# One transpose for both key blocks of an attention tile, split behind it by a triangular mask

## The chip, the core and the metric

The kernel runs on one core of one Trainium2 chip. The metric is the time of one execution on the device in microseconds (us); lower is better. The kernel before took 815.19 us, the median of three runs (814.88 to 815.65). One further execution was profiled; all views of the trace come from it.

The engines are named as in the profile: PE (matrix products and transposes; PEld is its loading of weights), DVE (the vector engine), ACT (the scalar engine), POOL (GpSimd) and SP (which issues transfers). Each engine works through its own list of instructions in order, and waits where an input or a free buffer is missing.

## The reference

Attention with a sliding window of 128 keys and 4 "sink" keys that are always seen, then a gated feed-forward block without a nonlinearity. Four sequences of 768 tokens, 8 heads of 64; model width 512, inner width 1536.

```python
scores = q @ k.T / sqrt(64)
keep   = (key < n_sink) | ((0 <= query - key) & (query - key < window))
a      = softmax(where(keep, scores, -1e9))
x      = (a @ v)                       # 8 heads side by side: 3072 x 512
out    = ((x @ w_a) * (x @ w_b)) @ w_out
```

## The kernel before, in words

**Tiling.** A q-tile is 128 queries, and a sequence has six of them. With a window of at most 128, the queries of tile t see the keys of key block t-1 ("A" below) and of block t ("B"), and the sinks. A tile of probabilities `p` is therefore 128 queries by 264 columns: 128 for A, 8 for the sinks, 128 for B. In A a key is in the window only where its place in its block is above the query's place in its tile; in B only where it is not above it. So at each of the 128 x 128 places at most one of A and B is not zero.

**Stages.** The work is cut into eight chunks (`CHUNKS`) of a sequence's q-tiles. For each chunk, `moe` computes the feed-forward block, and the attention of the next chunk is woven into it in small steps. The first two chunks use another path, `parts_exact`, in which the change touches nothing. The six others use `parts_split`, with three q-tiles each: three chunks hold the tiles 0 to 2 of a sequence ("first halves") and three the tiles 3 to 5 ("second halves"). With 8 heads that makes 24 units (head, tile) per chunk and 144 in all. A unit is in `late` when its tile is the third or a later one: one of three in a first half, all three in a second half, so 3 x 8 + 3 x 24 = 96 units.

**A unit, step by step** (lines of the kernel before): PE makes the scores (L396); DVE adds the mask and takes the row extreme (L401); ACT takes the exponential and its row sum (L403); DVE adds a small constant and inverts (L405, L406); ACT scales `p` (L407) and, in late units, copies the 8 sink columns out (L412). Two steps later PE transposes A and B, one instruction each (L428), into one PSUM tile `t`; ACT copies both to `pt` in the rounded format of the products (L431, called hi below), and DVE writes the remainder beside it (L432, lo). When a head's three units are there, PE multiplies them with the values (L444, `av`), five or seven products in the order of `GROUPS`; ACT and DVE add the two halves of the result into `xf` (L449 to L451). In each second half POOL prepares the next heads' operands (`ks`, `qh`, `ql`, `vv`: L322, L325), and in the feed-forward block it makes `gl` (L689).

**What sets the order.** A scheduler orders the program of each engine at build time, from its own estimates; at run time the order is fixed. Buffers that matter: four of `p`, one of `pt` for both hi and lo, one PSUM bank each for scores (`s`), transposes (`t`) and `av`.

## Time and profile before

| | before |
|---|---|
| median of 3 runs | 815.19 us |
| profiled execution | 814.39 us, of which the span of the trace is 812.5 us |
| PE busy | 788.8 us, 97% of the span |
| DVE, ACT, POOL busy | 53%, 59%, 47% |
| granted TensorE clock | 0.993 of full speed |
| attention of the six `parts_split` chunks | from 192 us to 712 us |

The attention of the second halves lies at 355 to 430, 450 to 525 and 637 to 712 us, that of the first halves at 192 to 249, 263.5 to 336 and 545.5 to 618 us. Line numbers (L428) are those of the kernel before. In a row, `out<-in` names tiles, then come sizes, the count, the summed busy time and the mean of one instruction in ns. A matrix instruction's time runs from its start to the landing of its last result, and the next one starts before that.

### The profile page before, as it was taken

To read this page: it belongs to the slowest core of one execution; us is meant where nothing else is said; L and a number is where in the kernel's file an instruction comes from. 1 tells how busy PE (TensorE), PEld (TensorE's weight loads), DVE (VectorE), ACT (ScalarE), POOL (GpSimd) and SP (SyncE) were. 2 spreads that over 40 slices of the span, in tenths; PEclk is the share of its full clock that TensorE was granted. 3 is DMA by queue.
4 is the path that set the end of the run, shared out by engine and by line. 5 is a ranking of instruction groups with operands and counts; after the bars stand their busy time and mean duration, and the time that the engine had idled before them with its cause. 6 is when DMAs were issued, how large, how long until landed. Compare 5 with 4: busy or idle time off the path is not lost.

```text
span 812.5 us, 13593 instructions
## 1 busy us (share of the span) xinstructions
PE 788.8 (97%) x4457; PEld 698.6 (86%) x4457; DVE 432.7 (53%) x1427; ACT 476.7 (59%) x1384; POOL 380.7 (47%) x483
## 2 busy tenths in 40 slices
PE   8997999999999999999999999999999999999995
PEld 5655777778989999999999999999999999999994
DVE  6889777834663555445654456535554456431001
ACT  5775665636774767467874677647765677631111
POOL 1248665673772564626653565506635366102110
PEclk9999899999999999999999999999999999999998
DMA  8866430031221133413323233221333132010001
GB/s 317 297 215 247 164 112 21 11 94 63 67 67 63 47 114 108 124 53 105 99 89 106 74 95 130 86 85 58 122 112 101 53 105 60 1 40 1 1 1 44
DMA packets 44784, 76.17 MB, mean 94 GB/s; under 512 B 4640, under 2 KB 24224, under 8 KB 44704
## 3 DMA queue, kind: packets, MB, share of 16 engines
q1 hardware_dynamic: 41648, 69.70, 26.5%
q10 hardware_dynamic: 3024, 5.51, 1.8%
q8 instruction: 37, 0.61, 0.3%
q14 instruction: 43, 0.35, 0.1%
q0 software_dynamic: 32, 0.00, 0.0%
HBM read 68.90 MB, written 6.29 MB: 93 GB/s over the span
## 4 chain that ended last, share of the span: by engine, by line
PE 85%; DVE 8%; ACT 3%; issue 2%; POOL 0%; DMA 0%; DVEq 0%; POOLq 0%; ACTq 0%
PE o L672 23%; PE a L663 23%; PE b L663 22%; PE t L428 4%; PE s L396 4%; PE av L444 3%; PE s L525 2%; PE av L579 1%; PE t L562 1%; PE t L579 1%; DVE p L539 1%; DVE wf_a L280 1%; DVE wf_a L278 1%; DVE g L684 1%; ACT p L403 1%
## 5 line engine op out<-in xcount | busy, mean ns | idle before, releaser
L663 PE MATMUL a<-xh,w_a 128*128 128x384 f32 (+2 forms) x768 | 218.9, 346 | 0.0
L663 PE MATMUL b<-xh,w_b 128*128 128x384 f32 (+2 forms) x768 | 215.3, 343 | 0.0
L672 PE MATMUL o<-w_o,gh 128*128 128x512 f32 x576 | 187.6, 406 | 0.0
L689 POOL TENSOR_TENSOR gl<-g,gh 128x384 fp32r<-128x384 f32 (+2 forms) x80 | 82.8, 1035 | 197.5 <-ACT gh L687 194.7
L663 PEld LDWEIGHTS a<-xh,w_a 128*128 128x128 f32 x768 | 138.8, 188 | 6.4 <-issue 1.5
L663 PEld LDWEIGHTS b<-xh,w_b 128*128 128x128 f32 x768 | 138.9, 188 | 4.5 <-issue 0.8
L684 DVE TENSOR_TENSOR g<-b,g 128x384 f32<-128x384 f32 (+2 forms) x96 | 53.4, 556 | 152.6 <-PE b L663 144.5
L663 PE MATMUL a<-xl,w_a 128*128 128x384 f32 (+2 forms) x384 | 129.3, 337 | 0.9 <-DVE xl L645 0.9
L663 PE MATMUL b<-xl,w_b 128*128 128x384 f32 (+2 forms) x384 | 129.1, 336 | 0.0
L672 PEld LDWEIGHTS o<-w_o,gh 128*128 128x128 f32 x576 | 104.6, 189 | 19.4 <-issue 1.0
L672 PE MATMUL o<-w_o,gl 128*128 128x512 f32 x288 | 114.0, 396 | 0.6 <-POOL gl L689 0.6
L687 ACT CAST gh<-g 128x384 fp32r<-128x384 f32 (+2 forms) x96 | 49.4, 514 | 80.9 <-DVE g L684 79.0
L680 ACT COPY g<-a 128x384 f32<-128x384 f32 (+2 forms) x96 | 45.2, 471 | 79.3 <-PE a L663 69.9
L407 ACT ACTIVATE p<-p,st 128x128 f32<-128x128 f32 (+1 forms) x144 | 71.4, 496 | 26.4 <-DVE st L406 25.5
L403 ACT ACTIVATE p<-p,st 128x128 f32<-128x128 f32 (+1 forms) x144 | 71.6, 497 | 8.4 <-DVE st L401 8.3
L663 PEld LDWEIGHTS a<-xl,w_a 128*128 128x128 f32 x384 | 72.5, 189 | 3.6 <-DVE xl L645 1.3
L663 PEld LDWEIGHTS b<-xl,w_b 128*128 128x128 f32 x384 | 72.5, 189 | 2.0 <-issue 0.3
L431 ACT CAST pt<-t 128x128 fp32r<-128x128 f32 (+1 forms) x144 | 50.4, 350 | 39.3 <-PE t L428 37.5
L432 DVE TENSOR_TENSOR pt<-t,pt 128x128 fp32r<-128x128 f32 (+1 forms) x144 | 57.2, 397 | 21.1 <-ACT pt L431 19.5
L672 PEld LDWEIGHTS o<-w_o,gl 128*128 128x128 f32 x288 | 54.3, 189 | 14.1 <-POOL gl L689 1.0
L322 POOL TENSOR_SCALAR qh<-qr 128x384 fp32r<-128x384 f32 x48 | 24.6, 512 | 75.8 <-PE s L396 48.1
L325 POOL TENSOR_TENSOR ks<-kr,ks 64x400 fp32r<-64x400 f32 (+1 forms) x48 | 57.6, 1200 | 3.9
(141 smaller groups left out, 1317.8 us busy)
## 6 DMA issues: line engine op xcount, KB each, us to landing
qr<-in_qT_dram SPq DMA_DIRECT2D x48, 192.0 KB, 2.6
raw_a<-in_wa_dram SPq DMA_DIRECT2D x12, 512.0 KB, 5.6
raw_b<-in_wb_dram SPq DMA_DIRECT2D x12, 512.0 KB, 6.3
raw_o<-in_wo_dram SPq DMA_DIRECT2D x12, 512.0 KB, 6.9
chk_a<-in_wa_dram SPq DMA_DIRECT2D x24, 256.0 KB, 2.8
chk_b<-in_wb_dram SPq DMA_DIRECT2D x24, 256.0 KB, 2.7
chk_o<-in_wo_dram SPq DMA_DIRECT2D x24, 256.0 KB, 2.7
out_dram<-os ACTq DMA_DIRECT2D x21, 256.0 KB, 2.1
```

The lines of the kernel that those rows point to most:

```text
L325: self.nc.gpsimd.tensor_tensor(o, i, high.bitcast(F32), op=ALU.subtract)
L396: nc.tensor.matmul(ps[:, :w], lhsT=q[:, i * P:(i + 1) * P], rhs=ks[:, c0:c0 + w], start=m == 0, stop=m == 1)
L403: nc.scalar.activation(p[:, :w], p[:, :w], AF.Exp, bias=st[:, 0:1], scale=-1.0, accum_out=st[:, 1:2])
L407: nc.scalar.mul(p[:, :w], p[:, :w], st[:, 3:4])
L431: nc.scalar.copy(hs, tp[:, :n, :])
L432: nc.vector.tensor_tensor(ls, tp[:, :n, :], hs.bitcast(F32), op=ALU.subtract)
L663: nc.tensor.matmul(ps[:, :n], lhsT=w[:, ksl], rhs=x[:, :n], start=kk == 0 and i == 0, stop=kk == NK - 1 and i == 2)
L672: nc.tensor.matmul(outs[i], lhsT=g[:, sl], rhs=w, start=j == 0 and k == 0, stop=j == NJ - 1 and k == 2)
L680: nc.scalar.copy(g[:, :n], pa[:, :n])
L684: nc.vector.tensor_tensor(g[:, :n], pb[:, :n], g[:, :n], op=ALU.mult)
L687: nc.scalar.copy(gh[:, :n], g[:, :n])
L689: e.tensor_tensor(gl[:, :n], g[:, :n], gh[:, :n].bitcast(F32), op=ALU.subtract)
```

## The change

In the 96 late units A and B are added before the transpose, which is possible since one of them is zero at each place. One transpose then carries both. Behind it they are separated: `ma` is a matrix of 0 and 1, with 1 where the key's place is above the query's; A is the transposed tile times `ma`, and B the transposed tile minus A. Both are written over `p`, in SBUF, and the hi copy and the lo remainder read them there and no longer in PSUM. The scaling is done on the 128 columns of the sum, and the 8 sink columns are scaled on their way out. The slots of `pt` are renumbered (`GROUPS`), the `av` products stay as many; `ma` is made once, by POOL, at the start.

```diff
-UNITS = ((0, 4, "BA"), (1, 2, "AB"), (3, 5, "AB"))
-GROUPS = ((0, 0, 2, 0), (1, 2, 2, 1), (2, 5, 0, 2), (-1, 4, 1, 0))
+GROUPS = ((0, 1, 2, 0), (1, 3, 2, 1), (2, 5, 0, 2), (-1, 0, 1, 0))
...
+        nc.gpsimd.memset(self.ma, 1.0)
+        nc.gpsimd.affine_select(out=self.ma, in_=self.ma, pattern=[[-1, P]], base=0, channel_multiplier=1,
+                                compare_op=ALU.is_gt, fill=0.0)
...
-            nc.scalar.mul(p[:, :w], p[:, :w], st[:, 3:4])
             state[h, i] = p
-            if i in late:
-                if h % 4 == 0:
-                    sc[h // 4, i] = self.at.tile([P, 4, NS], F32, tag=f"sc{i}", name=f"sc{u}", bufs=2)
-                nc.scalar.copy(sc[h // 4, i][:, h % 4, :], p[:, P:P + NS])
+            if i not in late:
+                nc.scalar.mul(p[:, :w], p[:, :w], st[:, 3:4])
+                return
+
+            own = p[:, P + NS:]
+            nc.vector.tensor_tensor(own, p[:, :P], own, op=ALU.add)
+            if h % 4 == 0:
+                sc[h // 4, i] = self.at.tile([P, 4, NS], F32, tag=f"sc{i}", name=f"sc{u}", bufs=2)
+            nc.scalar.mul(own, own, st[:, 3:4])
+            nc.scalar.mul(sc[h // 4, i][:, h % 4, :], p[:, P:P + NS], st[:, 3:4])
...
-            for k, o in enumerate(order):
-                nc.tensor.transpose(tp[:, k, :], parts[o], self.ident)
-            n = len(order)
-            hs, ls = (self.pt_split()[:, part, c1:c1 + (n - 1) * (c2 - c1) + 1:c2 - c1, :] for part in range(2))
-            nc.scalar.copy(hs, tp[:, :n, :])
-            nc.vector.tensor_tensor(ls, tp[:, :n, :], hs.bitcast(F32), op=ALU.subtract)
+            c = 0 if t else 1
+            hs, ls = (self.pt_split()[:, part, 2 * i + c:2 * i + 2, :] for part in range(2))
+            if i in late:
+                nc.tensor.transpose(tp[:, 0, :], p[:, P + NS:], self.ident)
+                ab = p[:, :2 * P].rearrange("p (c q) -> p c q", q=P)
+                nc.vector.tensor_tensor(ab[:, 0, :], tp[:, 0, :], self.ma, op=ALU.mult)
+                nc.vector.tensor_tensor(ab[:, 1, :], tp[:, 0, :], ab[:, 0, :], op=ALU.subtract)
+            else:
+                parts = [p[:, :P], p[:, P + NS:]] if t else [p[:, :P]]
+                for k, part in enumerate(parts):
+                    nc.tensor.transpose(tp[:, k, :], part, self.ident)
+                ab = tp[:, :2 - c, :]
+            nc.scalar.copy(hs, ab)
+            nc.vector.tensor_tensor(ls, ab, hs.bitcast(F32), op=ALU.subtract)
```

The order on DVE at head 2 of a second half (names are sequence-start tile 3, head, unit; the last number is a buffer's). Before, from the row extreme of the first unit of head 2 to that of the third:

```order
L401 ISA p_3_2_0_4486,st_3_2_0_4487<-s_3_2_0_4483,mg 128x264
L401 ISA st_3_2_0_4487 128x1
L432 TENSOR_TENSOR pt<-t_3_0_0_4330,pt 128x256
L405 TENSOR_SCALAR st_3_2_0_4487<-st_3_2_0_4487 128x1
L406 RECIPROCAL st_3_2_0_4487<-st_3_2_0_4487 128x1
L401 ISA p_3_2_1_4510,st_3_2_1_4511<-s_3_2_1_4507,mg 128x264
```

The same stretch on DVE in the changed kernel:

```order
L405 ISA p_3_2_0_4531,st_3_2_0_4532<-s_3_2_0_4528,mg 128x264
L405 ISA st_3_2_0_4532 128x1
L436 TENSOR_TENSOR p_3_1_1_4437<-t_3_0_0_4368,ma 128x128
L437 TENSOR_TENSOR p_3_1_1_4437<-t_3_0_0_4368,p_3_1_1_4437 128x128
L409 TENSOR_SCALAR st_3_2_0_4532<-st_3_2_0_4532 128x1
L417 TENSOR_TENSOR p_3_2_0_4531<-p_3_2_0_4531 128x128
L410 RECIPROCAL st_3_2_0_4532<-st_3_2_0_4532 128x1
L444 TENSOR_TENSOR pt<-p_3_1_1_4437,pt 128x256
L405 ISA p_3_2_1_4557,st_3_2_1_4558<-s_3_2_1_4554,mg 128x264
```

Between one row extreme and the next stand three more instructions: the masked product and the difference (L436, L437) of an earlier unit, and the sum of A and B (L417) of the present one. The lo remainder (L444) has moved from the second place to the last.

On ACT at the same head before, from the cast of the feed-forward block to the exponential of the second unit:

```order
L687 CAST gh_2_4467<-g_2_4425 128x384
L403 ACTIVATE p_3_2_0_4486,st_3_2_0_4487<-p_3_2_0_4486,st_3_2_0_4487 128x264
L407 ACTIVATE p_3_2_0_4486<-p_3_2_0_4486,st_3_2_0_4487 128x264
L412 COPY sc_3_0_0_4289<-p_3_2_0_4486 128x8
L431 CAST pt<-t_3_0_0_4330 128x2x128
L403 ACTIVATE p_3_2_1_4510,st_3_2_1_4511<-p_3_2_1_4510,st_3_2_1_4511 128x264
```

The same on ACT in the changed kernel, on to the exponential of the third unit:

```order
L699 CAST gh_2_4512<-g_2_4468 128x384
L407 ACTIVATE p_3_2_0_4531,st_3_2_0_4532<-p_3_2_0_4531,st_3_2_0_4532 128x264
L443 CAST pt<-p_3_1_1_4437 128x256
L420 ACTIVATE p_3_2_0_4531<-p_3_2_0_4531,st_3_2_0_4532 128x128
L421 ACTIVATE sc_3_0_0_4324<-p_3_2_0_4531,st_3_2_0_4532 128x8
L407 ACTIVATE p_3_2_1_4557,st_3_2_1_4558<-p_3_2_1_4557,st_3_2_1_4558 128x264
L443 CAST pt<-p_3_1_2_4473 128x256
L420 ACTIVATE p_3_2_1_4557<-p_3_2_1_4557,st_3_2_1_4558 128x128
L421 ACTIVATE sc_3_0_1_4337<-p_3_2_1_4557,st_3_2_1_4558 128x8
L692 COPY g_3_4592<-a_3_4579 128x384
L309 ACTIVATE chk_o_0_4451,chk<-chk_o_0_4451 128x256
L309 ACTIVATE chk_o_1_4453,chk<-chk_o_1_4453 128x256
L407 ACTIVATE p_3_2_2_4597,st_3_2_2_4598<-p_3_2_2_4597,st_3_2_2_4598 128x264
```

The hi copy (L443) has moved behind the exponential of a later unit. The exponentials of the first and of the third unit stand behind work of the feed-forward block and of the weight check (L699, L692, L309).

More of the change, by code (lines that the diff above doesn't have):

```diff
@@ L213, in consts @@
         self.m0 = cp.tile([P, P], F32, name="m0")
+        self.ma = cp.tile([P, P], F32, name="ma")
         self.m1 = cp.tile([P, SW], F32, name="m1")
@@ L257, in pt_split @@
         if self.pt is None:
-            self.pt = self.cp.tile([P, 2, 7, P], F32R, tag="pt", name="pt")
+            self.pt = self.cp.tile([P, 2, 6, P], F32R, tag="pt", name="pt")
         return self.pt
@@ L421, in transposes @@
             tp = tps[0][:, 2 * (n % 2):2 * (n % 2) + 2, :]
-            c1, c2, order = UNITS[i]
-            parts = {"A": p[:, :P], "B": p[:, P + NS:]}
-            if t == 0:
-                parts["B"] = p[:, :P]
-                order = "B"
-            for k, o in enumerate(order):
-                nc.tensor.transpose(tp[:, k, :], parts[o], self.ident)
-            n = len(order)
-            hs, ls = (self.pt_split()[:, part, c1:c1 + (n - 1) * (c2 - c1) + 1:c2 - c1, :] for part in range(2))
-            nc.scalar.copy(hs, tp[:, :n, :])
-            nc.vector.tensor_tensor(ls, tp[:, :n, :], hs.bitcast(F32), op=ALU.subtract)
+            c = 0 if t else 1
[12 more added lines that the diff above has]
+            nc.vector.tensor_tensor(ls, ab, hs.bitcast(F32), op=ALU.subtract)
         def av(h):
```

## Prediction

> **What bounds the kernel now.** I read the page first, then the busy times by stage, then single rows of one head.
>
> ```profile
> span 812.5 us, 13593 instructions
> PE 788.8 (97%) x4457; PEld 698.6 (86%) x4457; DVE 432.7 (53%) x1427; ACT 476.7 (59%) x1384; POOL 380.7 (47%) x483
> PE 85%; DVE 8%; ACT 3%; issue 2%; POOL 0%; DMA 0%; DVEq 0%; POOLq 0%; ACTq 0%
> ```
>
> PE is busy for 97% of the span and makes 85% of the chain that ended last. The whole span hides stages, so here are the six in which the changed units run: first halves at 192, 263.5 and 545.5 us, second halves at 355, 450 and 637 us. Columns: length, then busy us (instructions) of PE, PEld, DVE, ACT and POOL, the clock, DMA.
>
> ```profile
> 192.00:249.00 57.00, 55.14 (x406) 51.19 (x404) 34.29 (x147) 41.12 (x132) 40.22 (x60) 1.00 0.22 64
> 263.50:336.00 72.50, 72.43 (x428) 67.50 (x428) 40.26 (x161) 49.43 (x160) 40.54 (x56) 1.00 0.29 90
> 355.00:430.00 75.00, 74.78 (x451) 70.11 (x450) 42.80 (x161) 54.62 (x176) 44.30 (x56) 1.00 0.30 91
> 545.50:618.00 72.50, 72.44 (x429) 67.52 (x428) 40.26 (x161) 49.50 (x160) 40.60 (x56) 1.00 0.30 90
> 637.00:712.00 75.00, 74.95 (x452) 70.30 (x451) 41.80 (x164) 52.42 (x164) 38.61 (x48) 1.00 0.17 49
> ```
>
> From 263 us on PE idles under 0.3 us per stage: here it is the bound, and time taken from it is gained, as long as no other engine takes its place. DVE is at 57% (42.80 of 75), but it works in order and with waits in between; its room is what this prediction turns on.
>
> **PE: 96 transposes fewer.** A transpose must be priced by the spacing of starts, not by its duration.
>
> ```profile
> 360.98 0.39 PE L672 MATMUL o<-w_o,gh 128*128 128x512 f32 x1
> 361.21 0.38 PE L428 MATMUL t<-ident,p 128*128 128x128 f32 x2
> 361.35 0.48 PE L672 MATMUL o<-w_o,gh 128*128 128x512 f32 x1
> 361.66 0.39 PE L672 MATMUL o<-w_o,gl 128*128 128x512 f32 x1
> ```
>
> The second view is that of the line's own instructions; its three numbers are the shortest, median and longest in ns:
>
> ```profile
> L428 PE MATMUL t<-ident,p x264: 270/273/332, 195.1 to 709.8; 128*128 128x128 f32 x132
> ```
>
> The pair took 0.38 us and one takes 273 ns, so the second starts 0.107 us behind the first. Check: from 361.21 to 361.66 stand two transposes and one 512-column product, whose own spacing is 0.23 (360.98 to 361.21); 0.45 - 0.23 leaves 0.22 for two. I take 0.108: 96 x 0.108 = **10.4 us**, 2.6 in each second half (24 units), 0.86 in each first half (8).
>
> The Trainium skill ("TensorE: Matmul & The Clock Gate", Part 4: PE-mode transpose) gives about 275 ns for a transpose inside a kernel. By that figure the saving would be an estimated 26 us; the trace agrees with it as a duration and shows that the next instruction does not wait for it.
>
> **ACT: no cost.** The scaling shrinks from 264 to 128 columns, the hi copy now reads SBUF; the nearest 256-column ACT row on SBUF is the weight check's (L305).
>
> ```profile
> L407 ACT ACTIVATE p<-p,st 128x264 f32<-128x264 f32 x120 | 61.8, 515 | 21.6 <-DVE st L406 20.7 <-DVE pt L432 0.5
> L407 ACT ACTIVATE p<-p,st 128x128 f32<-128x128 f32 x24 | 9.5, 398 | 4.8 <-DVE st L406 4.8
> L431 ACT CAST pt<-t 128x256 fp32r<-128x256 f32 x120 | 44.2, 368 | 38.7 <-PE t L428 37.3 <-DVE g L684 0.4
> L305 ACT ACTIVATE chk_o<-chk_o 128x256 f32<-128x256 f32 x24 | 10.4, 435 | 4.1 <-DVE chk L303 4.1
> L687 ACT CAST gh<-g 128x384 fp32r<-128x384 f32 x72 | 37.0, 514 | 67.7 <-DVE g L684 67.5
> ```
>
> 515 - 398 = 0.12 us less, 435 - 368 = 0.07 more: a wash. Making `ma` (two POOL instructions behind the first 3 us, POOL then idle until its first copy) costs nothing; if DVE had to wait for it, it would be under 1 us.
>
> **DVE: three instructions more per late unit.** Each is 128 wide; the nearest row is the 128-wide remainder.
>
> ```profile
> L432 DVE TENSOR_TENSOR pt<-t,pt 128x128 fp32r<-128x128 f32 x24 | 6.7, 281 | 0.7 <-ACT pt L431 0.4
> L432 DVE TENSOR_TENSOR pt<-t,pt x144: 261/424/427, 195.7 to 710.5; 128x256 fp32r<-128x256 f32 x120, 128x128 fp32r<-128x128 f32 x24
> 372.20 0.43 DVE L401 CUSTOM_DVE_ANT_0 p<-s,mg 128x264 f32<-128x264 f32 x1 [0.67 <-PE s L396]
> 372.56 0.08 DVE L401 DVE_READ_ACCUMULATOR2_ANT st<- 128x1 f32 x1
> 372.82 0.42 DVE L432 TENSOR_TENSOR pt<-t,pt 128x256 fp32r<-128x256 f32 x1 [0.18 <-ACT pt L431]
> 373.16 0.41 DVE L303 TENSOR_REDUCE chk<-chk_o 128x1 f32<-128x256 f32 x1
> 374.75 0.43 DVE L401 CUSTOM_DVE_ANT_0 p<-s,mg 128x264 f32<-128x264 f32 x1 [0.72 <-PE s L396]
> 375.95 0.15 DVE L405 TENSOR_SCALAR st<-st 128x1 f32<-128x1 f32 x1 [0.76 <-ACT p L403]
> ```
>
> Neighbours that don't depend on each other overlap by 0.07 to 0.08 us (372.82 + 0.42 against 373.16). So sum of A and B 0.21, product 0.28, difference 0.28 (it waits for the product): 0.75 us per unit, 18 us per second half. Alone that fits into the 32 us that DVE idles there.
>
> **The wait behind POOL.** Before, the remainder (L432) read one input from PSUM; its 144 instances never took over 427 ns, though POOL is busy 44.3 of 75 us. Now it reads two inputs from SBUF, and so does the sum. What two-SBUF-input instructions cost beside POOL is seen in the weight stage:
>
> ```profile
> L294 DVE TENSOR_TENSOR w_a<-wf_a,w_a x12: 669/684/1783, 47.7 to 170.3; 128x512 fp32r<-128x512 f32 x12
> 119.85 0.95 DVE L294 TENSOR_TENSOR w_o<-wf_o,w_o 128x512 fp32r<-128x512 f32 x1
> 131.90 1.64 DVE L294 TENSOR_TENSOR w_o<-wf_o,w_o 128x512 fp32r<-128x512 f32 x1
> 118.93 1.31 POOL L282 TENSOR_TENSOR wf_o<-wf_o,raw_o 128x512 int32<-128x512 int32 x1 [0.17 <-ACT raw_o L279]
> 131.68 1.30 POOL L282 TENSOR_TENSOR wf_o<-wf_o,raw_o 128x512 int32<-128x512 int32 x1 [0.39 <-ACT raw_o L279]
> ```
>
> Undisturbed it takes 0.68. At 131.90 POOL's instruction still had 1.08 us to run (131.68 + 1.30), and the excess is 1.64 - 0.68 = 0.96; at 119.85 it had 0.39 and the excess is 0.27. Both are the rest of POOL's instruction less 0.12: DVE stands until POOL's is through. The Trainium skill ("SBUF — State Buffer", Who interferes with whom) has this as a rule: a DVE instruction with two SBUF inputs and a GpSimd one that reads SBUF share a port, and the second to come stands for the whole of the first. It would also hold POOL behind DVE, which no row here shows.
>
> In the second halves POOL's instructions are shorter:
>
> ```profile
> L325 POOL TENSOR_TENSOR ks<-kr,ks 64x536 fp32r<-64x536 f32 x8 | 10.8, 1344 | 0.7
> L689 POOL TENSOR_TENSOR gl<-g,gh 128x384 fp32r<-128x384 f32 x9 | 9.1, 1013 | 18.9 <-ACT gh L687 18.5 <-POOL ks L325 0.3
> L325 POOL TENSOR_TENSOR ql<-qr,qh 128x384 fp32r<-128x384 f32 x7 | 7.1, 1015 | 0.4
> L325 POOL TENSOR_TENSOR vv<-vr,vv 128x256 fp32r<-128x256 f32 x7 | 5.2, 738 | 0.6
> ```
>
> At a random moment the rest of POOL's present instruction is the sum of (count x duration squared) over twice the stage: these rows give 35, POOL's other ones (0.40 to 0.63 us each) about 6; 41 / 150 = 0.27 us, less 0.12 x 0.59 = **0.20 us** for each of the two instructions. Bounds: 0 (they fall into POOL's gaps) and 0.30 (the sum and the remainder mostly meet `ks`, `ql` and `gl`).
>
> **A head on DVE, added up.** With the changed order: the row extreme 0 to 0.35; product and difference to 0.93; the small sum (L405 before) not before 1.20, since the exponential stands between (374.75 to 375.95); the sum of A and B at 1.28 plus its wait of 0.20; the inverse 0.21 behind it and the remainder 0.10 behind that, at 1.8, plus its own 0.20; its successor 0.35 later. That is 2.35 us a unit with the wait behind POOL, 1.95 without, so 7.05 or 5.85 a head. The rest of DVE's work (products of the feed-forward block, `xf`, weight check, sinks) is 42.80 less 24 units of 1.0 (0.35 + 0.35 + 0.3), over 8 heads: 2.3. Of the waits for ACT, one or two exponentials a head now stand behind a cast or the check's squares (0.51, or 2 x 0.44, rows above): +0.6. In all **9.95 us, or 8.75 without the wait behind POOL**. PE needs for a head:
>
> ```profile
> 360.74 0.28 PE L396 MATMUL s<-ks,qh 128*128 128x264 f32 x1
> ...
> 374.55 0.93 PE L444 MATMUL av<-pt,vv 128*128 128x256 f32 x7
> ...
> 416.71 0.28 PE L396 MATMUL s<-ks,qh 128*128 128x264 f32 x1
> ```
>
> From the first scores of head 1 to those of head 7 are 55.97 us, 9.33 a head, and 9.0 without three transposes. So DVE would be 0.95 too slow a head; since some of its extras slip into the waits I counted, I take 0.7. PE then stands at `av`, whose remainder ends 1.3 us early today (372.82 + 0.42 to 374.55), so the first 1.3 us of delay are free.
>
> **Sum.** Second half: -2.6 + 8 x 0.7 - 1.3 = +1.7, three of them +5.1. First halves have 8 late units and ample room on DVE (40.26 of 72.5 plus 10): -0.86 each, less some 0.4 for the longer path to `av`: -1.4. Together +3.7 on the profiled 814.39 (span 812.5 and 1.9 around it): 818.1. The median of the runs is 0.8 above that execution, so I forecast **818 to 819, say 818.5 us**.
>
> **Rivals.** *PE's gain stands (faster).* If DVE seldom meets POOL, a head costs 8.75 against 9.0, and what is left is the path of each stage's first units, longer by the sum of A and B (0.28 x 6, about 1.5): 815.2 - 10.4 + 1.5 = 806. For it: POOL idles 30 of 75 us, and PE does not stand before DVE has lost 1.3 us. It decides where the wait is below 0.1 us. *DVE is the bound outright (much slower).* At 0.30 a wait and all extras in line a head costs 10.5, 1.5 over PE's: 8 x 1.5 - 2.6 - 1.3 = +8 per second half, 815.2 + 24 - 1.4 = 838. Against it: the longer a head, the smaller POOL's share. *A wash.* At 0.5 us too slow a head a second half comes to 8 x 0.5 - 2.6 - 1.3 = +0.1, and with the first halves' -1.4 it is 814. That the transposes are not saved is out: the order shows one per late unit.
>
> **How the numbers follow.** Forecast (816.8 to 825) 0.40, PE's gain stands (804 to 812) 0.31, a wash (812 to 816.8) 0.17, DVE the bound (over 825) 0.12. What the measurement tells from no change is 0.2%, 813.6 to 816.8. Slower: 0.40 + 0.12 = 0.52; same: 0.15 of the wash; faster: 0.31 + 0.02 = 0.33. The range is 805 to 829, which leaves 0.05 below and 0.09 above; the forecast's own is 815 to 825.
>
> **What would show it.** Right: PE's transposes x168 and its idle time in the second halves up from 0.2 to some 5 us each, ended by the remainder; DVE over 90% busy there; the remainder and the sum with medians near 0.42 and 0.28 but means 0.2 above. Wrong: means without excess (no wait behind POOL), or PE at 99% and second halves 2.6 us shorter.

## The result and the profile after

| | before | after |
|---|---|---|
| device time, median (range) | 815.04 us (814.04 to 815.65) | 833.87 us (832.14 to 835.30) |
| profiled execution, its span | 814.39, 812.5 us | 833.8, 832.1 us |

The changed kernel is slower: ratio 1.023 (95% interval 1.0213 to 1.0247), 18.8 us. The forecast was 818.5, slower by 3.5.

The page of the changed kernel, its span, its busy times and its chain by engine:

```profile
span 832.1 us, 13720 instructions
PE 795.4 (96%) x4361; PEld 693.0 (83%) x4361; DVE 524.0 (63%) x1715; ACT 475.6 (57%) x1384; POOL 386.9 (47%) x485
PE 65%; DVE 20%; ACT 10%; issue 3%; DMA 1%; POOL 1%; ACTq 0%; DVEq 0%; POOLq 0%
```

PE has the 96 transposes fewer, and DVE is busy for 91 us more, of which some 42 us are waits (below); PE's share of the chain fell from 85 to 65%, DVE's rose from 8 to 20%. The six stages of the changed kernel (the same stretches as in the prediction, shifted; columns length, PE, PEld, DVE, ACT, POOL, clock, DMA):

```profile
192.50:250.00 57.50, 54.99 (x384) 50.05 (x383) 41.68 (x168) 40.39 (x130) 40.14 (x59) 0.97 0.21 58
266.70:340.00 73.30, 72.33 (x420) 66.69 (x418) 47.92 (x185) 49.32 (x160) 40.99 (x55) 1.00 0.29 89
359.40:436.00 76.60, 72.78 (x406) 65.64 (x405) 63.62 (x228) 52.65 (x171) 44.69 (x53) 0.98 0.28 85
460.20:535.00 74.80, 71.71 (x407) 64.54 (x406) 62.50 (x226) 52.17 (x169) 43.62 (x53) 1.00 0.28 85
559.20:633.00 73.80, 72.79 (x420) 66.83 (x419) 48.53 (x185) 49.53 (x160) 41.36 (x56) 1.00 0.29 89
652.30:730.00 77.70, 75.71 (x428) 68.04 (x427) 62.88 (x236) 51.77 (x164) 39.66 (x48) 1.00 0.16 47
```

The prediction speaks of six stages and shows five; the sixth, a second half, was before the change:

```profile
450.00:525.00 75.00, 74.78 (x451) 70.13 (x450) 42.81 (x161) 54.50 (x176) 44.00 (x57) 1.00 0.28 89
```

PE idles 2 to 4 us in a second half (0.1 to 0.2 before) and 1 to 2.5 us in a first half (0.1 to 1.9 before), yet DVE is busy for 84% of a stage at most (62.50 of 74.80). From the first scores of each stage to those of the next (the last: to the last product), in us:

| stage | before | after | change | forecast | all the work, no wait (e14, below) |
|---|---|---|---|---|---|
| first halves | 71.5, 91.7, 91.7 | 74.1, 92.7, 93.1 | +2.6, +1.0, +1.4 | -0.5 each | 69.8, 90.8, 90.8 |
| second halves | 95.2, 95.2, 167.0 | 100.8, 99.0, 169.7 | +5.6, +3.8, +2.7 | +1.7 each | 93.7, 93.4, 165.9 |

That is +17.1 of the spans' 19.6 us; 0.4 lies ahead of the first stage and 2.0 behind the last product (more on that at the end).

The view of each line's own instructions (shortest, median, longest in ns) of the changed kernel, for the sum, the remainder, the product and the difference:

```profile
L417 DVE TENSOR_TENSOR p<-p x96: 274/410/1628, 197.4 to 723.1; 128x128 f32<-128x128 f32 x96
L444 DVE TENSOR_TENSOR pt<-p,pt x96: 397/426/1555, 201.3 to 728.9; 128x256 fp32r<-128x256 f32 x96
L436 DVE TENSOR_TENSOR p<-t,ma x96: 260/281/292, 200.2 to 727.7; 128x128 f32<-128x128 f32 x96
L437 DVE TENSOR_TENSOR p<-t,p x96: 264/291/293, 200.5 to 728.1; 128x128 f32<-128x128 f32 x96
```

The two with one input in PSUM vary by at most 32 ns; the two with both inputs in SBUF by more than 1 us. By the groups of instructions their means are 528 and 605 ns. I call what they take above 274 and 424 ns the **wait**: 24.3 us over the 96 sums, 17.3 over the 96 remainders, 41.7 us in all, a mean of 0.22 (the estimate was 0.20). 33 of these 192 instructions, with over 0.5 us each, make 25 of the 41.7 us. What PE's product with the values waited for, from the view of its own line (us, times; PE and its loading of weights, PEld, are added up there):

```profile
L456 PE MATMUL av<-pt,vv x288: 219/281/389, 200.9 to 730.2; 128*128 128x256 f32 x120, 128*128 128x128 f32 x24
its engine sat idle before it (us, times) until:
  DVE pt L444: 17.9, 33
```

From the list of all waits (us, times, longest), the two parts of this, and PE's wait at the scores for the sinks' remainder `sct`, which DVE makes once per four heads:

```profile
PEld av L456 <- DVE pt L444: 12.6, 26, 2.3
PE av L456 <- DVE pt L444: 5.3, 7, 2.1
PE s L400 <- DVE sct L474: 2.7, 4, 1.6
```

The first two overlap in time, so 17.9 us are more than PE itself stood there.

One such place, in order of time (start, length, engine; the idle time before in brackets):

```profile
427.74 0.63 POOL L326 TENSOR_SCALAR ks<-kr 64x536 fp32r<-64x536 f32 x1 [5.18 <-DMA kr<-in_kT_dram]
428.16 1.32 DVE L417 TENSOR_TENSOR p<-p 128x128 f32<-128x128 f32 x1
428.34 1.00 POOL L701 TENSOR_TENSOR gl<-g,gh 128x384 fp32r<-128x384 f32 x1
428.42 0.52 PE L456 MATMUL av<-pt,vv 128*128 128x256 f32 x3
...
429.41 1.31 POOL L329 TENSOR_TENSOR ks<-kr,ks 64x536 fp32r<-64x536 f32 x1
429.48 1.52 DVE L444 TENSOR_TENSOR pt<-p,pt 128x256 fp32r<-128x256 f32 x1
...
431.06 0.68 PE L456 MATMUL av<-pt,vv 128*128 128x256 f32 x4 [2.12 <-DVE pt L444]
```

The sum of one unit stands through the rest of POOL's `ks` and through `gl`; the next POOL instruction begins at its end, and the remainder of an older unit, next on DVE, stands through that one too. PE had the last four products of `av` next in its own order and stood for 2.12 us. And PE's clock pays once more; the stretches ahead of and behind 432.43:

```profile
429.02:432.43 3.41, 1.37 (x10) 1.37 (x11) 2.73 (x9) 1.61 (x5) 3.08 (x5) 1.00 0.00 0
432.43:435.84 3.41, 3.41 (x13) 3.31 (x12) 3.10 (x10) 1.67 (x6) 2.15 (x2) 0.50 0.24 77
```

After 3.41 us in which PE worked for 1.37, the granted clock was 0.50 for the next 3.41 us; the same came at 227.61, where PE had stood 1.62 us at the scores for an `sct` that comes behind a sum of 1.63 us on DVE. If PE gets half as much done in such a stretch, 1.7 us are lost each time, 3.4 us in all; this is an estimate.

In the six stages PE idles for some 11 us more than before. That and the clock are not the whole loss: PE's busy time rose too, from 788.8 to 795.4 us, with 96 transposes fewer. A matrix instruction's time runs to the landing of its result, so a short stall between two of them can count as busy; how much of the loss lies there isn't shown.

### The profile page after: what moved, and what is told of

The parts are those of the page before. It is cut to its first block, busy times and chain, and to the rows that moved or that the text cites. A ratio compares the mean times of both kernels' runs of the same rounds, so it can differ in the third digit from the quotient of the medians.

```text
span 832.1 us, 13720 instructions
## 1 busy us (share of the span) xinstructions
PE 795.4 (96%) x4361; PEld 693.0 (83%) x4361; DVE 524.0 (63%) x1715; ACT 475.6 (57%) x1384; POOL 386.9 (47%) x485
## 3 DMA queue, kind: packets, MB, share of 16 engines
q1 hardware_dynamic: 41648, 69.70, 26.2%
## 4 chain that ended last, share of the span: by engine, by line
PE 65%; DVE 20%; ACT 10%; issue 3%; DMA 1%; POOL 1%; ACTq 0%; DVEq 0%; POOLq 0%
PE a L675 18%; PE b L675 17%; PE o L684 17%; ACT p L407 4%; DVE pt L444 3%; DVE p L417 3%; PE s L400 2%; PE av L456 2%; DVE g L696 2%; PE s L537 2%; ACT gh L699 1%; PE av L591 1%; DVE xf L462 1%; PE t L574 1%; DVE st L409 1%
## 5 line engine op out<-in xcount | busy, mean ns | idle before, releaser
L675 PEld LDWEIGHTS b<-xh,w_b 128*128 128x128 f32 x768 | 140.6, 191 | 4.7 <-issue 0.8
L699 ACT CAST gh<-g 128x384 fp32r<-128x384 f32 (+2 forms) x96 | 49.3, 513 | 100.6 <-DVE g L696 98.0
L692 ACT COPY g<-a 128x384 f32<-128x384 f32 (+2 forms) x96 | 45.4, 473 | 82.9 <-PE a L675 72.6
L407 ACT ACTIVATE p<-p,st 128x128 f32<-128x128 f32 (+1 forms) x144 | 71.2, 495 | 24.4 <-DVE st L405 23.9
L444 DVE TENSOR_TENSOR pt<-p,pt 128x256 fp32r<-128x256 f32 x96 | 58.0, 605 | 8.2 <-ACT pt L443 7.4
L420 ACT ACTIVATE p<-p,st 128x128 f32<-128x128 f32 x96 | 38.6, 402 | 37.7 <-DVE st L410 36.9
L456 PE MATMUL av<-pt,vv 128*128 128x256 f32 (+1 forms) x288 | 50.9, 292 | 7.5 <-DVE pt L444 5.3
L456 PEld LDWEIGHTS av<-pt,vv 128*128 128x128 f32 x288 | 40.9, 188 | 16.4 <-DVE pt L444 12.6
```

The lines of the kernel that those rows point to most:

```text
L407: nc.scalar.activation(p[:, :w], p[:, :w], AF.Exp, bias=st[:, 0:1], scale=-1.0, accum_out=st[:, 1:2])
L420: nc.scalar.mul(own, own, st[:, 3:4])
L444: nc.vector.tensor_tensor(ls, ab, hs.bitcast(F32), op=ALU.subtract)
L456: nc.tensor.matmul(ps[:, cols], lhsT=vv[:, blk, :], rhs=m, start=n == 0, stop=n == len(products) - 1, skip_group_check=True)
L675: nc.tensor.matmul(ps[:, :n], lhsT=w[:, ksl], rhs=x[:, :n], start=kk == 0 and i == 0, stop=kk == NK - 1 and i == 2)
L692: nc.scalar.copy(g[:, :n], pa[:, :n])
```

## The experiments

Every ratio is to the kernel before, timed beside the run on the same chip. The runs come from several chips, and the kernel before has medians of 814.3 to 816.5 us there, so a difference between two runs' medians can be off by some 2 us. "Wait" is the total as defined above. Theories: T1, waits behind POOL on an in-order DVE; T2, only the longer way of one unit from transpose to remainder; T3, the saving on PE is smaller than priced.

| run | median us | ratio to before (95%) | wait us |
|---|---|---|---|
| after | 833.87 | 1.0230 (1.0213 to 1.0247) | 41.7 |
| e1 gain alone | 806.97 | 0.9880 (0.9851 to 0.9909) | 0 |
| e3 no sum | 811.85 | 0.9946 (0.9930 to 0.9962) | 17.3 |
| e2 remainder from PSUM | 820.85 | 1.0060 (1.0038 to 1.0081) | 23.8 |
| e4 both | 809.45 | 0.9916 (0.9884 to 0.9948) | 0 |
| e8 sum as product by 1.0 | 821.65 | 1.0076 (1.0045 to 1.0107) | 27.4 |
| e6 one product | 821.54 | 1.0093 (1.0074 to 1.0113) | 25.4 |
| e5 dead transpose | 850.24 | 1.0428 (1.0403 to 1.0454) | 51.1 |
| e7 merged scores | 805.75 | 0.9894 (0.9873 to 0.9914) | 0 |
| e9 sum from PSUM | 830.75 | 1.0187 (1.0163 to 1.0211) | 14.6 |
| e10 e2 and e9's idea | 816.84 | 1.0020 (1.0004 to 1.0036) | 2.9 |
| e11 gain and sum | 826.54 | 1.0132 (1.0109 to 1.0155) | 34.4 |
| e12 sum on POOL | 896.08 | 1.0988 (1.0968 to 1.1008) | 12.1 |
| e13 after, sum as reduction | 813.21 | 0.9969 (0.9956 to 0.9982) | 15.5 |
| e14 e2, sum as reduction | 807.99 | 0.9893 (0.9863 to 0.9923) | 0 |
| e15 e11, sum as reduction | 807.16 | 0.9882 (0.9853 to 0.9910) | 0 |
| e16 sum behind the scaling | 829.00 | 1.0164 (1.0136 to 1.0192) | 37.0 |
| e18 complete, without waits | 808.96 | 0.9932 (0.9902 to 0.9961) | 0 |
| e19 e14 and dead transpose | 818.34 | 1.0025 (1.0012 to 1.0038) | 0 |

**e1, the saving by itself.**

```diff
+            if i in late:
+                nc.tensor.transpose(tp[:, 0, :], parts["B"], self.ident)
+                src = tp[:, 0, :].unsqueeze(1).to_broadcast([P, 2, P])
```

> The kernel before with one transpose less per late unit (96 in all) and nothing else added: the A and B slots both take the transpose of B's probabilities (the part of the computation that is replaced: A's probabilities). Three theories of why the changed kernel is 18.8 us slower than before (833.87 against 815.04). T1: the saving is there as priced (96 x 0.108 = 10.4 us), and DVE, which works in order and has 0.75 us more per late unit and waits behind POOL of 0.25 and 0.185 us, ends the remainders late. T2: the saving is there, but what costs is only the longer row of steps from the transpose to the remainder of one unit (product, difference, copy, remainder), not DVE's load or its waits behind POOL. T3: the saving itself is small, since PE had to stand for something else in those places anyway. T1 and T2 expect 803.5 to 806.5 us here, T3 over 809.

Measured 806.97: just above the range of T1 and T2, and 2 us below T3's. The ratio of 0.988 makes 9.8 us of 815.04, and its interval 7.4 to 12.1. The price of 0.108 us per transpose, 10.4 us in all, fits, and T3 falls; e19 tests the price again.

**e3, e2, e4: the sum, the remainder, both.**

```diff
-            nc.vector.tensor_tensor(own, p[:, :P], own, op=ALU.add)          # e3, e4
...
-                nc.vector.tensor_tensor(ab[:, 0, :], tp[:, 0, :], self.ma, op=ALU.mult)
-                nc.vector.tensor_tensor(ab[:, 1, :], tp[:, 0, :], ab[:, 0, :], op=ALU.subtract)
+                nc.vector.tensor_tensor(ab[:, 0, :], tp[:, 1, :], self.mab[:, 0, :], op=ALU.mult)   # e2, e4: ab is tp
+                nc.vector.tensor_tensor(ab[:, 1, :], tp[:, 1, :], self.mab[:, 1, :], op=ALU.mult)
```

> The changed kernel without the sum of A and B (left out of the computation: A's probabilities; B's alone are scaled, transposed and separated). DVE loses 96 instructions of 528 ns mean (50.6 us, of it 24 us wait behind POOL). The sum does not lie between the transpose and the remainder of a unit. T1: what is late on DVE gets earlier by 0.5 us a unit, 12 us in a second half, more than the stall there: 808 to 816 us. T2: the way from the transpose to the remainder is as long as before, so at most 1 us per second half is gained: 829 to 834.

> The changed kernel, with A and B separated back into PSUM by two masked products (0.28 us each, as the product and the difference now), so that the copy and the remainder read PSUM as they did before: as many instructions in the same order, but the remainder has one input in SBUF and should not stand behind POOL. T1: the remainder falls from a mean of 605 to about 425 ns, 17 us less on DVE and 0.18 us less on each unit's way to the product with the values; of the some 6 to 8 us of stalls in each second half a third goes: 824 to 829 us. T2: only the 0.18 us of the last unit of each head counts, 48 heads in the split stages: at most 5 us less where they stand at all, 829 to 833. No wait behind POOL at all in the remainder (its mean stays at 600): 833 to 835.

> The changed kernel without the sum (left out as in the run above) and with the separation back into PSUM by two masked products: none of the added instructions reads two inputs from SBUF, so no wait behind POOL is left; only 0.56 us of products per late unit is added to the kernel before. T1: 805 to 810 us, the saving of 10.4 less a few stalls. T2: the way from the transpose to the remainder is still 0.56 us longer, which every second half's eight heads pay: 814 to 830.

Measured 811.85, 820.85 and 809.45: 22, 13 and 24 us less than the changed kernel. T2 expected 829 or more of the first and 814 or more of the third, and falls. The first and the third lie in T1's ranges. In e2 the remainder (all its forms) is back to the range it had before:

```profile
L446 DVE TENSOR_TENSOR pt<-t,pt x144: 266/416/427, 196.2 to 718.4; 128x256 fp32r<-128x256 f32 x120, 128x128 fp32r<-128x128 f32 x24
L419 DVE TENSOR_TENSOR p<-p x96: 280/447/1643, 197.4 to 712.6; 128x128 f32<-128x128 f32 x96
```

With 0.2 us off a remainder e2 gained more than any theory said (824 to 829 by T1); e3 couldn't tell the sum's work from its wait.

**e8 and e6: the sum's wait, the products' work.**

```diff
-            nc.vector.tensor_tensor(own, p[:, :P], own, op=ALU.add)
+            nc.vector.tensor_scalar(own, p[:, :P], 1.0, None, op0=ALU.mult)                          # e8
...
+                nc.vector.tensor_tensor(ab, tp[:, 1, :].unsqueeze(1).to_broadcast([P, 2, P]), self.mab, op=ALU.mult)   # e6, for e2's two
```

> The changed kernel with the sum replaced by a product of A with 1.0 in the same place, which reads one input from SBUF instead of two (left out of the computation: B's probabilities). As many DVE instructions in the same order; the sum's wait behind POOL (528 - 274 = 0.25 us each, 24 us in all) should go, and the instruction itself should take 0.2 to 0.28 us. Leaving the sum out altogether gave 22 us (833.87 to 811.85). If DVE's time counts as such, whatever it is spent on, about half of that comes back here, 24 to 31 of 50.6 us: 820 to 824. If it is the waits that matter most (they are long ones, up to 1.6 us, and come just when the remainder is due): 812 to 818. If only the instruction's place counts: 830 to 834.

> The changed kernel with both masked products made by one 256-wide instruction, from one transposed slot read twice back into the two slots of the PSUM bank (result as the reference's). Against the run with two products into PSUM (820.85) DVE has one instruction less per late unit: about 0.42 instead of 0.59 us, 16 us in all, and the way from the transpose to the remainder is shorter by 0.17. The sum and its wait behind POOL stay. DVE's load decides: 814 to 818. Only the way counts: 818 to 820. PE's waits for the bank of the transposes (12.8 us there) should shrink to under 7.

e8 did not do what it was meant to. Its stand-in has one input in SBUF and waited all the same:

```profile
L417 DVE TENSOR_SCALAR p<-p x96: 212/260/1512, 197.7 to 712.2; 128x128 f32<-128x128 f32 x96
```

The Trainium skill ("SBUF — State Buffer", Who interferes with whom) says why it may: such a product of one SBUF tile can run in a mode that takes both port pairs of DVE, one of them POOL's. The trace agrees. Its 820 to 824 for "DVE's time counts as such" came in, but since the stand-in waited, 821.65 tells only that 14 us less of DVE time in the sum and the remainder, work and waits together, brought 12 us. e6 missed: 424 ns for the one product against 0.59 us for two takes 16 us of DVE work away, PE's loading waits 7.0 instead of 12.8 us for the bank of the transposes, and 821.54 is no better than e2's time. **Plain DVE work was worth nothing there**, which speaks for waits and against load.

**e5: the transposes put back.**

```diff
                 nc.tensor.transpose(tp[:, 0, :], p[:, P + NS:], self.ident)
+                nc.tensor.transpose(tp[:, 1, :], p[:, :P], self.ident)
```

> The changed kernel with a second transpose per late unit put back (of A's half of the sum's tile, into the second slot of the bank, never read). Tells whether PE's time still counts in the changed kernel: if PE were the bound outside of a few stalls, 96 x 0.108 = 10.4 us come on top: 842 to 845. If in the second halves PE stands for the remainder at nearly every head, 7.8 of the 10.4 us fall into those stalls, and only the first halves' 2.6 us and the half-clock stretches remain: 833 to 838.

850.24, 16.4 us more: neither figure. The waits rose from 41.7 to 51.1 us, and the longest sum is the reason for a place of its own:

```profile
511.74 0.63 POOL L326 TENSOR_SCALAR ks<-kr 64x536 fp32r<-64x536 f32 x1
512.17 3.34 DVE L417 TENSOR_TENSOR p<-p 128x128 f32<-128x128 f32 x1
512.34 1.00 POOL L329 TENSOR_TENSOR ql<-qr,qh 128x384 fp32r<-128x384 f32 x1
513.32 0.40 POOL L326 TENSOR_SCALAR vv<-vr 128x256 fp32r<-128x256 f32 x1
513.69 0.99 POOL L702 TENSOR_TENSOR gl<-g,gh 128x384 fp32r<-128x384 f32 x1
514.65 0.71 POOL L329 TENSOR_TENSOR vv<-vr,vv 128x256 fp32r<-128x256 f32 x1
515.44 1.31 POOL L329 TENSOR_TENSOR ks<-kr,ks 64x536 fp32r<-64x536 f32 x1
```

DVE stood through the rest of a `ks` (to 512.37) and through four POOL instructions behind it, each of which starts 0.02 to 0.03 us before the last one's end, and was done just behind the first gap (515.36 to 515.44). The clock was halved in five stretches, one of them of double length, instead of two (leaving out the one near 80 us, which the kernel before has too): by the estimate above some 10 us instead of 3.4. e19 below takes the waits out of this experiment.

**e7: merging ahead of the exponential.**

```diff
+                nc.vector.copy_predicated(ps[:, P + NS:], self.mg[:, :P].bitcast(I32), ps[:, :P])
-            nc.vector.tensor_tensor_reduce(out=p[:, :w], in0=ps[:, :w], in1=m, scale=-0.125, ...
+            nc.vector.tensor_tensor_reduce(out=p[:, f:w], in0=ps[:, f:w], in1=m, scale=-0.125, ...   # f is P for late units
-            nc.vector.tensor_tensor(own, p[:, :P], own, op=ALU.add)
```

> The two key blocks are merged before the exponential: a predicated copy on DVE takes A's scores over B's where the triangular mask says so, PSUM to PSUM, so that the row extreme, the exponential and the scaling run over 136 columns instead of 264, the sum is gone, and the separation is the one 256-wide product into PSUM (result as the reference's). No added instruction reads two inputs from SBUF. DVE gets the copy (0.28 to 0.4 us) and the product (0.42), and the row extreme loses some 0.1 us: about +0.6 to 0.7 us per late unit without any wait behind POOL, as in the run without the sum and with the products into PSUM (+0.59, 809.45). By load and waits: 806 to 812 us, faster than both kernels. If the longer way from the scores to the exponential counts (the copy ahead of the row extreme): 813 to 820.

The mask of these units is the larger of the two blocks' masks, element by element. 805.75, ratio 0.9894: the complete computation, and faster than both kernels (by 1.1% than the one before). The rows of the copy, the row extreme and the product:

```profile
L416 DVE COPY_PREDICATED s<-mg,s x96: 283/295/297, 195.2 to 695.1; 128x128 f32<-128x128 int32 x96
L417 DVE CUSTOM_DVE_ANT_0 p<-s,mg x96: 289/299/301, 195.6 to 695.4; 128x136 f32<-128x136 f32 x96
L447 DVE TENSOR_TENSOR t<-t,mab x96: 411/427/433, 199.7 to 700.8; 128x256 f32<-128x256 f32 x96
```

None of them varies by more than 22 ns.

**e9, e10, e11, e12: the sum elsewhere.**

```diff
+            nc.vector.tensor_tensor(own, tps[0][:, 2 * (n % 2) + 1, :], own, op=ALU.add)            # e9
+            a = tps[0][:, 2 * ((n + 1) % 2), :] if n > 2 else p[:, :P]                              # e10, on e2
+            nc.vector.tensor_tensor(own, a, own, op=ALU.add)
+                nc.vector.tensor_tensor(p[:, P + NS:], p[:, :P], p[:, P + NS:], op=ALU.add)          # e11, on e1
+            nc.gpsimd.tensor_tensor(own, p[:, :P], own, op=ALU.add)                                  # e12
```

> The changed kernel with the sum's second input taken from the unused slot of the transposes' PSUM bank, set to zero once per stage, instead of A in SBUF (left out of the computation: A's probabilities). As many DVE instructions in the same order and of the same kind; the sum now has one input in SBUF. The run with the product by 1.0 in its place didn't tell wait from work, since that instruction waited too (436 ns mean, 260 median, 1512 longest). If the sum's wait behind POOL is what costs: its mean falls from 528 to about 290 ns and 23 us of DVE time bring 15 to 20 us: 814 to 819. If the work costs (leaving the sum out brought 22 us): 826 to 832.

> The changed kernel with none of its three added instructions and no remainder standing behind POOL: the two masked products into PSUM, and the sum with its second input from the other half of the transposes' PSUM bank (left out of the computation: A's probabilities; an older unit's stand in for them). All the work of the change is there, 96 x (0.29 + 0.29 + 0.29) = 84 us more on DVE than before, and none of the waits. By the waits: 808 to 812 us, near the run without the sum (809.45). By the load on DVE, or the longer way: 816 to 821, as in the run whose sum still waits (820.85).

> The run with the gain alone (one transpose of B per late unit, nothing else added, 806.97 us; A's probabilities left out behind the sum) with only the sum of A and B added, two inputs from SBUF. Tells what one waiting instruction costs where DVE has 32 us of idle time per second half and nothing else is added. If each wait counts for what it lasts (24 us, at three quarters as in the run with the remainder from PSUM, 13 for 17): 818 to 826. If waits cost only where DVE is nearly full (two of them and the products together): 807 to 811.

> The changed kernel with the sum on POOL instead of DVE (result as the reference's). DVE loses 50.6 us, as in the run without the sum (811.85), but POOL gets some 96 x 0.4 = 38 us, its instructions come in order behind `ks`, `ql` and `gl` (up to 1.3 us each), the scaling waits for them, and the remainder meets POOL more often. If DVE alone matters: 812 to 815. If the sum comes late through POOL's queue: 820 to 835, with ACT's scaling ended by POOL's sum.

e9 (830.75) and e10 (816.84) came out in the ranges for work and load, against T1, though no sum waits in e9 (281 ns mean) and the waits are down to 14.6 and 2.9 us. But they don't tell wait from work: an input from the transposes' bank makes PE wait for the sum, and it put many other instructions in another order. How much of the two times each of these makes is not shown; e13 to e15 repeat the question in an unchanged order. PE's waits in e9 (us in total, times, longest):

```profile
PEld t L445 <- DVE p L421: 4.3, 16, 0.4
PEld t L438 <- DVE p L421: 3.4, 12, 0.7
```

e11 is plain: **the sum alone, on the kernel with the gain, costs 19.6 us**, though nothing else is added. Its sums waited 34.4 us, and DVE is busy for only 69% of its first second half (52.50 of the 76.10 us from 360.9 to 437). The rival that waits cost only on a nearly full DVE falls. e12 is the worst of all, far outside both expectations: ACT's scaling stood 117.5 us for POOL's sum, which queues behind POOL's long instructions:

```profile
ACT p L420 <- POOL p L417: 117.5, 70, 4.2
ACT gh L699 <- DVE g L696: 84.0, 79, 2.5
```

**e13, e14, e15: only the wait taken away.**

```diff
-            nc.vector.tensor_tensor(own, p[:, :P], own, op=ALU.add)
+            nc.vector.tensor_reduce(own[:, 0:1], p[:, :P], axis=AX.X, op=ALU.max)
```

> The changed kernel with the sum replaced by a row reduction of A's 128 columns into B's first column, in the same place and with the same order of all other instructions on every engine (left out of the computation: A's probabilities). In the changed kernel the reductions of the weight check (L307, 256 columns from SBUF) took 398 to 421 ns and never more, so they don't stand behind POOL; this one should take 0.27 to 0.29 us each time, as long as the sum without its wait. What is left of the change is all its work and the remainder's wait. If the sum's wait costs: 24 us of DVE time less, 812 to 819, near the run without the sum (811.85). If the sum's work, or its place ahead of the scaling costs: 829 to 834.

> The run with the remainder from PSUM (820.85) with the sum replaced by the same reduction, again with the order of everything else unchanged (left out: A's probabilities): all the work of the change and no wait behind POOL at all, without the detour of the earlier run that took the sum's input from the transposes' bank and made PE wait for the sum (816.84). If the waits are the whole loss: 808 to 811, as in the run without the sum (809.45). If the work or the place of the sum costs something of its own: 813 to 821.

> The run with the gain alone and the sum (826.54) with the sum replaced by the same reduction, in the same order (left out: A's probabilities). The sum alone had cost 19.6 us there. If that is its wait behind POOL: 807 to 810. If it is the extra instruction between the inverse and the scaling: 820 to 827.

The reduction against the sum in the same place, first in e13, then in e11 and e15:

```profile
L417 DVE TENSOR_REDUCE p<-p x96: 270/276/280, 197.1 to 702.8; 128x1 f32<-128x128 f32 x96
```

```profile
L408 DVE TENSOR_TENSOR p<-p x96: 279/548/2589, 197.0 to 718.5; 128x128 f32<-128x128 f32 x96
```

```profile
L408 DVE TENSOR_REDUCE p<-p x96: 274/276/280, 196.4 to 696.6; 128x1 f32<-128x128 f32 x96
```

As long as a sum without its wait, and never longer. By the Trainium skill ("SBUF — State Buffer", Who interferes with whom) a reduction never contends with POOL on this chip; these rows agree. The times: 833.87 to 813.21, 820.85 to 807.99, 826.54 to 807.16, each pair with the same work in the same order on every engine. So the sum's **wait** costs 20.7, 12.9 and 19.4 us (21.3, 13.6 and 20.4 by the ratios), and its work nothing that shows. e14 has all of the change's work, some 0.87 us per unit on DVE, and ends within 1 us of e1, the gain alone. The wait at `av` for the remainder, PE and PEld added up as above, is 17.9 us in the changed kernel, 9.9 in e13 and 0.9 in e14.

**e16: the sum behind the scaling.**

```diff
+            nc.scalar.mul(p[:, :w], p[:, :w], st[:, 3:4])
+            if i in late:
...
+                nc.vector.tensor_tensor(own, p[:, :P], own, op=ALU.add)
```

> The changed kernel with the sum behind the scaling instead of ahead of it (ACT scales all 264 columns as it did before and copies the sinks' columns; result as the reference's). ACT's scaling no longer waits for the sum (it waited 36.9 us in 60 places in the changed kernel), but the sum still stands behind POOL, and comes later. If ACT's standing behind the sum is what costs: 815 to 825. If it is DVE that stands, whatever waits for it: 830 to 840.

829.00, just under the second range, 4.9 us below the changed kernel. ACT's waits ahead of the scaling fell from 36.9 to 18.5 us, but those ahead of the exponential (L407) rose from 23.9 to 36.1. The waits behind POOL fell from 41.7 to 37.0, and no stretch at half clock is left in the stages, which alone is some 3.4 us. So most of the loss stays when ACT no longer stands for the sum ahead of the scaling; ACT's waits for DVE as a whole are not taken away here.

**e18: the change without its waits.**

```diff
+            ab = bass.AP(p.tensor, p.offset, [list(p.ap[0]), [1, P], [KB, 2]])
...
+            nc.vector.tensor_reduce(both, ab, axis=AX.X, op=ALU.add)
...
+                nc.vector.tensor_tensor(ab[:, 0, :], tp[:, 1, :], self.ma, op=ALU.mult)
+                nc.vector.scalar_tensor_tensor(out=ab[:, 1, :], in0=self.ma, scalar=0.5, in1=tp[:, 1, :],
+                                               op0=ALU.is_lt, op1=ALU.mult)
```

> The changed kernel's computation, complete, with no DVE instruction of the change that reads two inputs from SBUF: the sum of A and B is a reduction over pairs (one input of 128 x 2 with a stride, output in a tile of its own that the scaling reads), the separation goes back into PSUM with one mask (A = mask times T, B = (mask below 0.5) times T). Result as the reference's. The reduction reads 256 columns, 0.41 us by the weight check's, so DVE has some 96 x (0.41 + 0.29 + 0.29) = 95 us more work than before, 12 more than in the run with the shorter reduction (807.99), but no wait behind POOL. If the waits were the whole loss: 807 to 811, faster than before by 0.6 to 1%, as the saving alone. If DVE's plain work counts after all: 812 to 822.

808.96, ratio 0.9932 (0.9902 to 0.9961): the complete computation is faster than before, by 0.7%, as soon as no added instruction waits behind POOL, although DVE is as busy as in e13 (60.49 of 75 us there). The window 355 to 430 us of e18:

```profile
355.00:430.00 75.00, 74.55 (x438) 68.47 (x438) 61.08 (x235) 55.25 (x181) 46.05 (x58) 1.00 0.28 88
```

DVE is busy for 81% here, as in the changed kernel (83%), and PE idles 0.45 us instead of 3.8.

**e19: the transposes put back, without waits.**

```diff
+                nc.tensor.transpose(tp[:, 0, :], p[:, :P], self.ident)
```

> The run without any wait behind POOL (807.99: remainder from PSUM, sum replaced by the short reduction; A's probabilities left out) with a second, never used transpose per late unit put back, as in the run on the changed kernel where that cost 16.4 us instead of 10.4. With the waits gone PE is the bound and each transpose should cost its 0.108 us: 816 to 819. If it costs some 16 us here as well (823 to 826), the surplus there wasn't from the waits. If under 6 us, PE stands for something else here.

818.34, 10.35 us above e14 where 96 x 0.108 = 10.4 was expected (that it fits so closely is luck, with runs that vary by 2 us). So some 10 of e5's 16.4 us are the transposes, and the other 6 came with 9.4 us more of waits and some 7 us more lost to the clock.

**The rate.** Pairs that differ in little else: after and e14 26 us for 41.7 us of waits, e11 and e15 19.4 for 34.4, e2 and e14 12.9 for 23.8. Each us of DVE's waits costs 0.54 to 0.62 us of the end there. It is no constant: the remainder's alone (e13 and e14) cost 5.2 for 15.5, a third, and the sum's in the changed kernel (after and e13) 20.7 for 26.2, 0.79. The sum's waits alone cost 12.9 us and the remainder's alone 5.2, both together 25.9: one makes the other dearer. In the changed kernel and in e11 some 3.4 us of the cost are half clock, which e2, e13, e14 and e15 don't have in their stages.

## Why the prediction was wrong

- **PE's gain** (10.4 us): right. e1 has 9.8 by its ratio, e19 10.35. The estimate of 26 us from a transpose's duration by the Trainium skill ("TensorE: Matmul & The Clock Gate", Part 4) does not agree with either run.
- **ACT, a wash:** right for its durations. The scaling takes 402 ns and the copy 406; but the sinks' own scaling takes 285 ns where the copy took 196, which was not counted.
- **DVE, three instructions more:** right in size (281 and 288 ns; 276 as the stand-in of the sum) and in that they fit. By e14 they cost nothing that shows.
- **The wait behind POOL** (0.20 each): right on the mean, 0.25 for the sum and 0.18 for the remainder.
- **"A head on DVE, added up"** is the step that failed, and with it "the first 1.3 us of delay are free" and "ample room on DVE" in the first halves. It put the waits into a sum of DVE's time per head and set 9.95 us against PE's 9.0, as though a wait costs only where DVE's head is the longer one. In e11 DVE is busy for 69%, and the sum's waits cost 19.4 us; in e14 and e18 it is busy for 76 and 81% without waits, and nothing shows to be lost. The runs show in its place that DVE's waits cost by themselves, 0.5 to 0.8 us of the end for each us in most pairs, wherever they hold up something that PE needs next.
- **By size**, each against e14: the second halves lost 5.5 us each where 4.3 stood (7.1, 5.6 and 3.8), the first halves 4.3, 1.9 and 2.3 with 8 late units each, at 42 of 57.5 and 48 of 73 us busy, where 0.4 stood. Of the 15.7 us by which the profiled execution missed the forecast, the first halves make 7.3 and the second halves 3.6; 2.5 are that e14's stages got shorter by 7.9 us and not by 10.4, and 2.4 lie outside the stages. That the second halves came near is in part luck, since the step that gave the 4.3 was wrong.
- **Why so few us of waits cost so much** is argued, not shown by a run of its own: 33 of the 192 instructions make 25 of the 41.7 us, and two such waits in a row made PE stand for 2.12 us above. A mean of 0.22 us hides them. PE stood at `av`, as forecast, but also at the scores for `sct`.
- **The clock** was not in the sum: two stretches at 0.50, some 3.4 us, which are part of these losses (one in a first half, one in a second).
- **The rivals.** PE's gain stands needed waits under 0.1 us; runs without any have just that time (805.75 to 808.96, against 806). DVE the bound outright had the nearest time, but for a cause that isn't there.
- **What would show it:** 168 transposes, the remainder ahead of `av`, and the means held. PE's idle time in the second halves rose to 2 to 4 us, not 5; the sum's median was 0.41 us, not 0.28, so most sums waited. DVE over 90% busy did not come (81 to 84%): load wasn't the mechanism.

## What to carry to other kernels

An in-order engine that is busy for 60 to 80% can still hold up the bound engine: ask how long its longest instruction may stand, and who has the next place behind it, not only whether its work fits. Where DVE runs beside POOL, choose the form of an added instruction by where its inputs lie: one input from PSUM, or a reduction, kept its 0.28 or 0.42 us, two inputs from SBUF took up to 3.3. The input from PSUM must not be one that PE then waits for, as in e9 and e10. A wait of DVE that the estimate spreads evenly over a head should be priced by its long cases too; here a us of waits cost between 0.3 and 0.8 us, mostly about 0.6.

## What was not expected of the hardware

- One DVE instruction can stand through several of POOL's. The prediction took the rest of the one under way, as the Trainium skill has it ("SBUF — State Buffer", Who interferes with whom: the second to come stands for the whole of the first); in e5 it was that rest and four more in a row, 3.34 us, until POOL left a gap of 0.08. In the changed kernel three sums and one remainder stood for longer than the instruction under way, which had at most 0.23 us left there. Others that came as late, or met POOL without a gap (a sum at 209.36), got in behind that instruction; what decides stays open.
- The granted clock can fall to half though PE is not idle throughout. The Trainium skill ("TensorE: Matmul & The Clock Gate", Part 1) tells of an idle window of some 3.4 us; here PE had 1.37 and 1.79 us of work in the 3.41 us ahead of the two stretches of the changed kernel, and 0.89 to 1.54 ahead of four of the five in e5. It doesn't follow each time: behind 1.89 us of work in 3.41 the clock stayed full in e2 and e8, and in e12 also behind 1.51 and 1.78.
- Left open: the 2.0 us behind the last product. That end takes 8.1 us in the profiled execution before and 10.1 after, but also 10.5 in e1 and e14, which have no waits, and 9.1 in e7, so it doesn't come from them.
